# A four-token decode block in one pass: a bf16 turn for the last group, a norm without helper tiles, a projection by columns and half-row loads in two parts

## The chip, the cores and the metric

The kernel runs on one core of a Trainium2 chip. The metric is the device time in microseconds (us) of one execution. TensorE (PE in the profile) multiplies matrices, PEld is its loading of weights, DVE is VectorE, ACT is ScalarE, POOL is GpSimd, and SP issues nearly all transfers from device memory (HBM) into the on-chip memory (SBUF).

## What is computed

Four tokens (B=4, one position each) with D=448 go through the same two blocks twice:

```python
x = x + A(layernorm(x));  x = x + F(layernorm(x))
x = x + A(layernorm(x));  x = x + F(layernorm(x))

def A(x):      # 16 query heads, 8 K/V heads, Dh = 256, window of the last 2048 positions
    q = (x @ wq).reshape(B, Sq, Hq, Dh).transpose(0, 2, 1, 3)
    k = repeat(k_cache[:, :, Sk - W:, :], 2, axis=1)     # W = 2048; v alike
    p = softmax(einsum("bhqd,bhkd->bhqk", q, k) * Dh ** -0.5)
    return einsum("bhqk,bhkd->bhqd", p, v) ... .reshape(B, Sq, Hq * Dh) @ wo

def F(x):      # width 1792
    return (silu(x @ w_gate) * (x @ w_up)) @ w_down
```

Weights and caches are bf16 and the same for both layers. A K or V window of one token and one K/V head is 1 MB. All of them, with the weights, make 103.9 MB.

## The kernel before

**Data.** K and V come in units of 512 KB (half a window) into 34 slots of SBUF. What a list named HOLD names stays there for layer 1; the rest is loaded a second time. A list named WHOLE says which K windows come as one transfer of 1 MB instead of two. SLOTS gives the slot of each unit. wq lies in slots that become free for K and V when the last query projection is done. `load` issues the weights; the last 64 rows of wq, gate and up (rows 384 to 447) are read with `"r (h c) -> (r h) c"`: half h of row r goes to partition 2r+h, in one transfer of 128 partitions.

**Tokens and stages.** Tokens don't go through the layers together. A plan of 38 stages says which (token, layer, K/V head) are worked on next, mostly pairs of groups, so that one token's FFN and next query projection run while another token's windows stream in. A group is named by these three numbers: 312 is token 3, layer 1, head 2, the last one.

**A group** (`group`): DVE transposes K in blocks (`tr`, L856), PE computes the scores (L890) with a query that POOL has masked (`qe`, L896), DVE takes the maximum (L906), PE spreads it over partitions (L911), ACT computes the exponentials (L924), PE turns them (L937), ACT copies them (L946), PE sums them (`tot`, L954), DVE (L959) and POOL (L981) make the reciprocals, PE multiplies with V (`pv`, L968, 32 matmuls of 256 columns). Then o is turned: ACT copies it in bf16 (`oh`, L995), DVE writes high minus low parts (`oho`, L997), PE turns it with two bf16 matmuls (`flip`, L1003), and DVE divides (`oT`, L1013). The last group alone takes another way: ACT copies in fp32 (`ohf`, L984), and PE turns with two fp32 matmuls (`flipf`, L989, four passes in the trace).

**Output projection** (`out_proj`): by rows (`opr`, L1033), four matmuls of 448 columns into bank A, or by columns (`opc`, L1025), sixteen of one column for each token. The stages that finish a token take columns, the others rows. When a token is done, `rows` copies the rows of bank A out (`rowcp`, L773), adds and turns them with eight fp32 matmuls (`rturn`, L778) and a zero matmul (`clear`, L529), and `residual` adds to x.

**Norm** (`norm`, L532 to L561), 16 times: DVE sums the squares (`nv`), PE sums over partitions into Z2 (`nstat`, L541), DVE subtracts the mean (`nxn`, L545) and copies the statistics (`ncp`, L547), POOL computes the scale. For the 64 last features, PE multiplies column 3 of xn with a tile that doubles each partition (`nxe`, L549, tile `twice`), and DVE masks the result into xe (`nxe2`, L552, tile `par`): partition 2r+h holds feature 384+r in half h.

**Query projection** (`qproj`) and FFN follow on a norm. In the FFN by columns, gate and up (`guc3` with xn, `guc1` with xe, L720) go through ACT and DVE into `downc` (L756), which ends with a `clear` (L529).

**Order.** Each engine's order is written out by hand in SEQ_PE, SEQ_DVE, SEQ_ACT, SEQ_POOL and SEQ_SP, as numbers of operations. A "w1" in SEQ_PE is a filler: a matmul of zeros, 512 columns wide, into bank A (L1112). Planned durations (DUR) serve to place waits only. 317 fillers stand in PE's order.

**The tail.** After the last V window: PE's order is scores 312, pv 311, flip 310, spread 312, filler, opc 310, turn 312, flip 311, nxe of token 1, tot 312, filler, opr 311, pv 312, rturn 3, flipf 312, nstat of token 2, opc, nstat of token 3, filler, nxe of token 3, then the FFN of the last tokens by columns, and the output (`orow`, `ocp`, two small transfers).

Of the kernel before, what the change touches and what calls it, by code (L numbers as in the profile page):

```python
# [85 lines left out]
)  # L86
SEQ_DVE = (
# [21 lines left out]
)  # L109
SEQ_ACT = (  # L110
# [66 lines left out]
class Graph:  # L177
# [45 lines left out]
    def dma(self, nbytes, emit, sem, r=(), w=(), cells=(), run=4096):  # L223
        o = self.op(SP, "ld", emit, r=r, w=w)
        o.nbytes, o.cells, o.run = nbytes, cells, run
        if not cells:
            self._count(o, sem)
# [951 lines left out]
```

## Time and profile before

| what | value |
|---|---|
| median of three runs | 282.47 us (280.79 to 282.82) |
| profiled execution | 281.3 us |
| its span, first to last instruction | 279.4 us |
| mean granted TensorE clock | 0.964 |
| PE busy | 256.0 us (92%), 4796 matmuls |
| of it L1112 (fillers) | 96.2 us, 317 times, 399 ns each |
| DVE busy | 179.5 us (64%) |
| ACT, POOL busy | 61.8 us, 80.3 us |
| read from HBM | 103.91 MB, 372 GB/s over the span |

Busy times say how much an engine did, not that it was the bound; for that one looks at which wait ends last in a stretch. The profile shows a granted clock of 1.00 or 0.50 for TensorE in each stretch; a share in between is a mix of the two. A line's mean duration mixes both.

### The profile page before, as it was taken

What the parts mean: (1) busy time and instruction counts of PE and PEld (TensorE: products, weight loads), DVE (VectorE), ACT (ScalarE), POOL (GpSimd) and SP (SyncE); (2) the same over time, 40 slices, a digit from 0 to 9 for tenths busy, and PEclk for the clock granted to TensorE, in tenths of its full rate; (3) what the DMA queues carried; (4) which work ended last, traced back from release to release, by engine and by line L of the source; (5) the groups of instructions that cost most, each with busy time, mean ns of one, the idle gap of its engine ahead of it and who ended that gap; (6) DMA issues with size and microseconds to landing.
All of it is one profiled execution on the core that took longest, in us unless ns stands there. A gap on an engine that the chain in (4) does not pass through costs nothing. (4 is left out here: it accounts for less than half of the span.)

```text
span 279.4 us, 10832 instructions
## 1 busy us (share of the span) xinstructions
PE 256.0 (92%) x4796; PEld 149.3 (53%) x4796; DVE 179.5 (64%) x548; ACT 61.8 (22%) x173; POOL 80.3 (29%) x225
## 2 busy tenths in 40 slices
PE   3899799999999999999998889999998999999995
PEld 1333344334775554545555445655764577576684
DVE  4388644634603789668766978793898858489421
ACT  0003010101113222232223123134213212423301
POOL 1033230011121534315232333243153242423430
PEclk9999989999999999999999999999999999989857
DMA  7999999999999999999999999999999999999200
GB/s 282 428 419 420 413 409 409 395 394 406 401 394 409 396 412 410 412 401 361 409 401 420 418 412 409 393 369 412 414 420 402 405 400 382 392 414 412 115 2 2
DMA packets 26894, 104.61 MB, mean 374 GB/s; under 512 B 2652, under 2 KB 6752, under 8 KB 22880
## 3 DMA queue, kind: packets, MB, share of 16 engines
q1 hardware_dynamic: 26839, 103.92, 93.5%
q8 instruction: 37, 0.61, 0.9%
q14 instruction: 10, 0.07, 0.1%
q10 hardware_dynamic: 8, 0.00, 0.0%
HBM read 103.91 MB, written 0.00 MB: 372 GB/s over the span
## 5 line engine op out<-in xcount | busy, mean ns | idle before, releaser
L856 DVE STREAM_TRANSPOSE half<-half 128x1024 uint32<-128x1024 uint32 x88 | 106.6, 1228 | 9.3 <-DMA half<-in_A_k_cache_dram 9.2
L1112 PE MATMUL A<-identb,small 128*128 128x512 bf16 x317 | 96.2, 399 | 4.4 <-DVE A L424 4.4
L981 POOL TENSOR_TENSOR small<-small 128x2 f32<-128x2 f32 (+1 forms) x48 | 38.5, 804 | 54.1 <-DVE small L959 54.1
L968 PE MATMUL Y<-half,pT 128*8 128x256 bf16 (+1 forms) x1024 | 45.7, 281 | 3.1 <-DMA half<-in_A_v_cache_dram 1.0
L890 PE MATMUL S<-half,qe 128*8 128x128 bf16 (+1 forms) x1536 | 43.5, 241 | 0.6 <-DVE half L856 0.2
L1112 PEld LDWEIGHTS A<-identb,small 128*128 128x128 bf16 x317 | 27.6, 104 | 29.9 <-issue 12.5
L890 PEld LDWEIGHTS S<-half,qe 128*8 128x8 bf16 x1536 | 30.8, 85 | 10.9 <-issue 1.6
L924 ACT ACTIVATE po<-S,small 104x128 bf16<-104x128 f32 (+1 forms) x48 | 19.3, 402 | 68.7 <-DVE small L920 66.6
L896 POOL TENSOR_TENSOR qe<-qc,tiny 128x64 bf16<-128x64 bf16 x64 | 17.9, 292 | 45.6 <-PE S L890 29.1
L997 DVE SCALAR_TENSOR_TENSOR po<-po,small,Y 128x256 bf16<-128x256 bf16 x47 | 22.0, 468 | 13.3 <-ACT po L995 13.2
L968 PEld LDWEIGHTS Y<-half,pT 128*8 128x8 bf16 (+1 forms) x1024 | 20.3, 85 | 17.6 <-issue 6.9
L995 ACT ACTIVATE po<-Y 128x256 bf16<-128x256 f32 x47 | 18.0, 383 | 48.1 <-PE Y L968 33.2
L906 DVE TENSOR_REDUCE tiny<-S 104x1 bf16<-104x128 f32 (+1 forms) x48 | 15.6, 326 | 11.5 <-PE S L890 11.2
L557 POOL TENSOR_SCALAR st<-st 128x1 f32<-128x1 f32 x16 | 4.2, 264 | 58.5 <-DVE st L547 52.5
L946 ACT ACTIVATE pT<-Y 128x64 bf16<-128x64 f32 (+1 forms) x48 | 12.2, 258 | 27.8 <-PE Y L937 27.7
L1033 PE MATMUL A<-wo_sb,oT 128*4 128x448 bf16 x188 | 16.4, 353 | 0.9 <-DVE oT L1013 0.9
L920 DVE TENSOR_REDUCE small<-S 104x1 f32<-104x32 f32 x48 | 8.6, 180 | 10.4 <-PE S L914 8.3
L1013 DVE TENSOR_TENSOR oT<-Y,small 128x4 bf16<-128x4 f32 (+1 forms) x63 | 8.9, 153 | 7.7 <-PE Y L989 4.6
L911 PE MATMUL S<-small,identb 104*104 104x32 bf16 x48 | 10.1, 210 | 3.4 <-DVE small L459 2.0
L1060 POOL MEMSET oT<- 128x16 bf16 x38 | 4.1, 111 | 29.9 <-PE A L1033 23.2
L959 DVE TENSOR_REDUCE small<-Y 128x2 f32<-128x32 f32 (+1 forms) x48 | 9.2, 191 | 5.0 <-PE Y L954 4.8
L778 PE MATMUL Z<-small,wide 128*128 128x1 f32 (+1 forms) x80 | 10.9, 249 | 0.5 <-ACT wide L773 0.5
(136 smaller groups left out, 268.0 us busy)
## 6 DMA issues: line engine op xcount, KB each, us to landing
half<-in_A_v_cache_dram SPq DMA_DIRECT2D x87, 512.0 KB, 10.6
half<-in_A_k_cache_dram SPq DMA_DIRECT2D x28, 1024.0 KB, 10.6
half<-in_A_k_cache_dram SPq DMA_DIRECT2D x32, 512.0 KB, 6.7
wo_sb<-in_A_wo_dram SPq DMA_DIRECT2D x8, 448.0 KB, 13.5
half<-in_A_wq_dram SPq DMA_DIRECT2D x3, 1024.0 KB, 12.3
wd_sb<-in_B_w_down_dram SPq DMA_DIRECT2D x1, 1568.0 KB, 20.2
wg_sb<-in_B_w_gate_dram SPq DMA_DIRECT2D x1, 1344.0 KB, 15.7
wu_sb<-in_B_w_up_dram SPq DMA_DIRECT2D x1, 1344.0 KB, 17.8
```

Of the source, the lines that this page charges most:

```text
L856: return e.transpose(a, a)
L890: last = e.matmul(Sb[s_][qd:qd + 8, 0:32 * 2 * J], lhsT=qe[q_][:, P, ce, :, :].rearrange("p a n -> p (a n)"), rhs=keys(kcs[P], J * x, J, c ...
L896: g.op(POOL, "qe", lambda e, P=P, t=t, kvh=kvh: e.tensor_tensor(qe[q_][:, P, :, :, :], qc[t][:, kvh, :, :].unsqueeze(2).broadcast_to([128, ...
L906: g.op(DVE, f"max{n}", lambda e: e.tensor_reduce(pmax[s_][0:R, :], Sb[s_][0:R, 0:N], AX.X, ALU.max), r=(f"s{s_}",), w=(f"pmax{s_}",), bank ...
L924: return e.activation(praw[0:R, 0:128 * n].rearrange("p (g r l) -> p g r l", g=2 * n, l=2), Sb[s_][0:R, 0:128 * n].rearrange("p (l g r) -> ...
L946: g.op(SCA, f"pt{n}", lambda e: e.activation(pf, Yb[p_][:, 0:PW], ACT.Copy), r=(f"yp{p_}",), w=(f"pT{pt}",), bank=(f"Y{p_}",))
L968: last = e.matmul(Yb[p_][32 * gg:32 * gg + M, 256:512], lhsT=pT[pt][:, gg, 2 * a + hv, 4 * P:4 * P + M] if n == 2 else p1[:, gg % 2, 2 * a ...
L981: g.op(POOL, f"pow{n}", lambda e: e.tensor_tensor(ri[p_][:, 0:2 * n], rs[p_][:, 0:2 * n], expo[:, 1:1 + 2 * n], op=ALU.pow), r=(f"rs{p_}", ...
L995: g.op(SCA, "oh", lambda e: e.activation(oh[:, :], Yb[p_][:, 256:512], ACT.Copy), r=(f"y{p_}",), w=("oh",), bank=(f"Y{p_}",))
L997: g.op(DVE, "oho", lambda e: e.scalar_tensor_tensor(out=oh[:, :], in0=oh[:, :], scalar=lomask[:, 0:1], in1=Yb[p_][:, 256:512], op0=ALU.mul ...
L1033: last = e.matmul(Ab[32 * k:32 * k + B, 0:D], lhsT=oT[oi][:, k % 2, k // 2, :], rhs=wo_sb[:, 4 * kvh + k, :], start=False, stop=False, ski ...
L1112: return e.matmul(Ab[:, 0:512], lhsT=zero[:, 0:1].broadcast_to([128, 128]), rhs=identb[:, :].unsqueeze(1).broadcast_to([128, 4, 128]), sta ...
```

## The change

1. **o of the last group.** `ohf` and `flipf` are gone, and the last group takes `oh`, `oho` and `flip` like the others.
2. **Norm.** `nxe` and `nxe2` are gone from all 16 norms, with the tiles `twice` and `par`. DVE writes xe itself with two instructions (`nx1`, `nx2`) of 64 partitions and one column each, from x and Z2: feature 384+r in half h is now on partition 64h+r. xn has three columns. On the last norm DVE's order is nxn, ncp, nx1, nx2.
3. **Half rows.** To fit this, the last 64 rows of wq, gate and up are loaded as two transfers of 64 partitions each, one after the other on SP.
4. **Second-last stage** projects by columns (`opc`) instead of rows (`opr`).
5. **Query projection.** `qs` now masks and widens on DVE (128 columns for each token, before 32), and `qsel` takes 4 matmuls instead of 16.
6. **clear** stands first in `downc` and in the turn of x at the start, with start=True.
7. **Lists.** HOLD has v331 for v360, WHOLE has 106 and 112 for 001 and 110; SLOTS and all orders are written anew. SP's order of loads is else the same, and so are the bytes. SEQ_PE has 264 fillers. In the tail of PE's order, a filler stands behind spread 312, two behind flip 311, none behind tot 312; opr 311 is opc 311.

```diff
@@ load
+            if isinstance(src, tuple):
+                g.dma(nbytes, lambda e: [e.dma_start(dst[64 * h:64 * h + 64], src[h]) for h in range(2)], f"w{nw[0]}",
+                      w=(key,), run=run, parts=2)
...
+        def halves(src, n):
+            return src[384:448, 0:n], src[384:448, n:2 * n]
...
-        load(1 << 19, wq_sb[:, 3 * 4096:], A_wq[384:448, :].rearrange("r (h c) -> (r h) c", h=2), "wq3", 4096)
+        load(1 << 19, wq_sb[:, 3 * 4096:], halves(A_wq, 2048), "wq3", 4096)
...
-                load(229376, wsb[:, 3 * FF:], src[384:448, :].rearrange("r (h c) -> (r h) c", h=2), nm + "b", 1792)
+                load(229376, wsb[:, 3 * FF:], halves(src, 896), nm + "b", 1792)
@@ norm
-            vec("nxn", lambda e: e.tensor_scalar(xn[:, :, t], x[:, t, :], Z2[:, 0:1], None, op0=ALU.subtract),
+            vec("nxn", lambda e: e.tensor_scalar(xn[:, :, t], x[:, t, 0:3], Z2[:, 0:1], None, op0=ALU.subtract),
...
-            g.op(PE, "nxe", lambda e: e.matmul(Z2[:, 16:17], lhsT=twice[:, :],
-                                                    rhs=xn[:, 3, t:t + 1], start=True, stop=True, skip_group_check=True),
-                 r=(f"xn{t}", "twice"), w=("z2",), bank=("Z2",))
-            vec("nxe2", lambda e: e.tensor_tensor(xe[:, :, t], par[:, :], Z2[:, 16:17].broadcast_to([128, 2]), op=ALU.mult),
-                ("z2", "par"), (f"xe{t}",), ("Z2",))
+            for h in range(2):
+                vec(f"nx{1 + h}", lambda e, h=h: e.tensor_scalar(
+                    xe[64 * h:64 * h + 64, h, t:t + 1], x[64:128, t, 3:4], Z2[64:128, 0:1], None, op0=ALU.subtract),
+                    (f"x{t}", "z2"), (f"xe{t}",), ("Z2",))
@@ qproj
-            vec("qs", lambda e: e.tensor_copy(qS[:, 0:32 * n], Zb[:, 0:32 * n]), ("z",), ("wa",), ("Z",))
+            vec("qs", lambda e: e.tensor_tensor(
+                qS[:, 0:128 * n].rearrange("p (k c x) -> p k c x", c=4, x=4),
+                Zb[:, 0:32 * n].rearrange("p (k x) -> p k x", x=4).unsqueeze(2).broadcast_to([128, 8 * n, 4, 4]),
+                qmask[:, :].unsqueeze(1).unsqueeze(3).broadcast_to([128, 8 * n, 4, 4]), op=ALU.mult),
...
-                for c in range(4):
-                    for a in range(4):
-                        o = Z2[32 * a:32 * a + 32, 0:128 * n].rearrange("p (k c x) -> p k c x", c=4, x=4)[:, :, c, :]
-                        last = e.matmul(o, lhsT=identb[:, 32 * c:32 * c + 32], rhs=src, start=(c == 0), stop=(c == 3),
-                                        skip_group_check=True)
+                for a in range(4):
+                    last = e.matmul(Z2[32 * a:32 * a + 32, 0:128 * n], lhsT=rep32[:, :], rhs=qS[:, 0:128 * n], start=True,
+                                    stop=True, skip_group_check=True)
@@ group
-            if final:
-                g.op(SCA, "ohf", lambda e: e.activation(ohf[:, :], Yb[p_][:, 256:512], ACT.Copy), r=(f"y{p_}",),
-                     w=("oh", "praw"), bank=(f"Y{p_}",))
...
-                g.op(PE, "flipf", flipf, r=("oh", "praw", "oself"), w=(f"yp{p_}",), bank=(f"Y{p_}",))
@@ stages
-                out_proj(oi, ts, kvh, bool(full))
+                out_proj(oi, ts, kvh, bool(full) or si + 2 == len(plan()))
```

More of the change, by code (lines that the diff above doesn't have):

```diff
@@ L53 @@
 SEQ_PE = (
[32 rows of a table removed]
[29 rows of a table added]
 )
 SEQ_DVE = (
[21 rows of a table removed]
[21 rows of a table added]
 )
 SEQ_ACT = (
[8 rows of a table removed]
[8 rows of a table added]
 )
 SEQ_POOL = (
[9 rows of a table removed]
[9 rows of a table added]
 )
 SEQ_SP = (
[7 rows of a table removed]
[7 rows of a table added]
 )
 SLOTS = (
[4 rows of a table removed]
[4 rows of a table added]
 )
 DUR = dict(
-    i0=.24, i1=.5, fill0=.98, mz=.49, d1=.17, d2=.27, nstat=.45, nxe=.18, rv1=.19, rv2=.33, qmm3=1.2, qmm1=.5, qcp=.69,
-    qturn=.25, qsel=.28, rvh=.24, rvt=.28, gur3=1.2, gur1=.7, tanhr=.69, fturn=.26, downr=.93, ohf=.38, flipf=.42, fh=.23, ft=.29, guc3=1.26,
-    guc1=.6, tanhc=.27, downc=1.65, rowcp=.54, rturn=.35, orow=.25, xin=.26, tr=1.24, qe=.29, sc1=.85, sc2=1.5, sch=1.2, max1=.29,
+    i0=.24, i1=.5, fill0=.98, mz=.49, d1=.17, xcp=.17, d2=.27, nstat=.45, rv1=.19, rv2=.33, qmm3=1.2, qmm1=.5, qcp=.69,
+    qturn=.25, qsel=.25, rvh=.24, rvt=.28, gur3=1.2, gur1=.7, tanhr=.69, fturn=.26, downr=.93, fh=.23, ft=.29, guc3=1.26,
+    guc1=.4, tanhc=.27, downc=1.7, rowcp=.54, rturn=.4, orow=.25, xin=.26, tr=1.24, qe=.29, sc1=.85, sc2=1.5, sch=1.2, max1=.29,
     max2=.42, spread=.3, negm=.18, exp1=.36, exp2=.47, turn1=.26, turn2=.35, pt1=.22, pt2=.33, tot1=.19, tot2=.23,
     sum1=.18, sum2=.23, pv=.5, pow1=.7, pow2=1.0, oh=.38, oho=.47, flip=.2, oT=.16, opc=.56, opr=.45, oz=.11, nw=.16,
-    nv=.16, nxn=.23, ncp=.15, nxe2=.15, qs=.2, qc=.28, ffa=.68, ffb=.75, fht=.18, fca=.23, fcb=.23, fcw=.22, st=.1, fx=.15, rowsub=.62,
+    nv=.16, nxn=.2, ncp=.15, nx1=.15, nx2=.15, qs=.2, qc=.28, ffa=.68, ffb=.75, fht=.18, fca=.23, fcb=.23, fcw=.22, st=.1, fx=.15, rowsub=.62,
     rowadd=.15, resid=.15, oxb=.16, ocp=.25, ng1=.26, ng2=.3, ng3=.57, fw=.45, ld=.05)
@@ L221, in op, with dma @@
         return o
-    def dma(self, nbytes, emit, sem, r=(), w=(), cells=(), run=4096):
+    def dma(self, nbytes, emit, sem, r=(), w=(), cells=(), run=4096, parts=1):
         o = self.op(SP, "ld", emit, r=r, w=w)
@@ L226, in dma, with _count @@
         if not cells:
-            self._count(o, sem)
+            self._count(o, sem, parts)
         return o
-    def _count(self, o, sem):
+    def _count(self, o, sem, parts=1):
         o.dsem = sem
-        self.dcount[sem] = self.dcount.get(sem, 0) + 16
+        self.dcount[sem] = self.dcount.get(sem, 0) + 16 * parts
         o.dval = self.dcount[sem]
@@ L355, in build @@
         identb = sb("identb", [128, 128], BF16)
-        twice = sb("twice", [128, 128], BF16)
-        tiny = sb("tiny", [128, 16 + NS], BF16)
-        onesb, qmask, osel, rsel = tiny[:, 0:1], tiny[:, 2:6], tiny[:, 6:10], tiny[:, 10:14]
-        par = tiny[:, 14:16]
-        pmax = [tiny[:, 16 + s:17 + s] for s in range(NS)]
-        tsel = sb("tsel", [128, 4, B], BF16)
+        rep32 = sb("rep32", [128, 32], BF16)
+        tiny = sb("tiny", [128, 14 + NS], BF16)
+        onesb, qmask, osel = tiny[:, 0:1], tiny[:, 2:6], tiny[:, 6:10]
+        pmax = [tiny[:, 14 + s:15 + s] for s in range(NS)]
+        tsel = identb[:, :].rearrange("p (j x) -> p j x", j=4)[:, :, 0:B]
         selt = [sb(f"selt{h}", [128, 4, 12], BF16) for h in range(2)]
@@ L427, in build @@
         XN = tuple(f"xn{t}" for t in range(B))
-        g.op(DVE, "fill0", c_fill, w=("onesf", "expo", "qmask", "zero") + XN +
+        g.op(DVE, "fill0", c_fill, w=("onesf", "expo", "qmask", "zero") + XE +
              tuple(f"acc{t}" for t in range(B)) + tuple(f"row{t}" for t in range(B)), bank=("A",))
@@ L528, in clear @@
         def clear(e, out, m):
-            return e.matmul(out, lhsT=zero[:, 0:1].broadcast_to([128, 64]), rhs=identb[:, 0:m], start=False, stop=True,
-                            skip_group_check=True)
+            return e.matmul(out, lhsT=zero[:, 0:1].broadcast_to([128, 64]), rhs=identb[:, 0:m], start=True, stop=False,
+                     skip_group_check=True)
         def norm(t, x, summed=True):
-            s, si, k = st[:, t, :], sti[:, t, :], f"st{t}"
+            s, k = st[:, t, :], f"st{t}"
             if not summed:
@@ L752, in down @@
                 k, last = 0, None
+                clear(e, Zb[0:64, 3 * cw:4 * cw], cw)
                 for cc in range(4):
@@ L759, in down @@
                         k += 1
-                return clear(e, Zb[0:64, 3 * cw:4 * cw], cw)
+                return last
             g.op(PE, "downc", down, r=WIDE + ("wd", "zero"), w=("z",), bank=("Z",))
@@ L799, in x_in @@
         def x_in(e):
+            clear(e, Zb[0:64, 12:16], 4)
             for cc in range(4):
                 q = 64 * (cc // 3)
-                e.matmul(Zb[q:128, 4 * cc:4 * cc + 4], lhsT=xio[0:B, 128 * cc:128 * cc + 128 - q], rhs=identb[0:B, 0:B],
+                last = e.matmul(Zb[q:128, 4 * cc:4 * cc + 4], lhsT=xio[0:B, 128 * cc:128 * cc + 128 - q], rhs=identb[0:B, 0:B],
                          start=(cc == 0), stop=(cc == 3), skip_group_check=True)
-            return clear(e, Zb[0:64, 12:16], 4)
+            return last
         g.op(PE, "xin", x_in, r=xio_k + ("identb", "zero"), w=("z",), bank=("Z",))
-        g.op(DVE, "d1", lambda e: e.tensor_copy(xs[:, :, :], Zb[:, 0:16].rearrange("p (c t) -> p t c", t=B)),
+        g.op(DVE, "xcp", lambda e: e.tensor_copy(xs[:, :, :], Zb[:, 0:16].rearrange("p (c t) -> p t c", t=B)),
              r=("z",), w=tuple(f"xs{t}" for t in range(B)) + tuple(f"x{t}" for t in range(B)), bank=("Z",))
@@ new lines, in group, with flip @@
+            g.op(SCA, "oh", lambda e: e.activation(oh[:, :], Yb[p_][:, 256:512], ACT.Copy), r=(f"y{p_}",),
+                 w=("oh",), bank=(f"Y{p_}",))
+            g.op(DVE, "oho", lambda e: e.scalar_tensor_tensor(
+                out=oh[:, :], in0=oh[:, :], scalar=lomask[:, 0:1], in1=Yb[p_][:, 256:512], op0=ALU.mult,
+                op1=ALU.subtract), r=(f"y{p_}", "oh", "lomask"), w=("oh",), bank=(f"Y{p_}",))
+            def flip(e):
+                for dh in range(2):
+                    last = e.matmul(Yb[p_][:, 2 * n * dh:2 * n * dh + 2 * n],
+                                    lhsT=oh[:, :].rearrange("p (m e) -> p e m", e=2)[:, dh, :],
+                                    rhs=osel[:, 0:2 * n], start=dh == 0, stop=dh == 1, skip_group_check=True)
+                return last
@@ L1008, in group @@
+            g.op(PE, "flip", flip, r=("oh", "osel"), w=(f"yp{p_}",), bank=(f"Y{p_}",))
             yo = Yb[p_][:, 0:4 * n].rearrange("p (d P n) -> p d P n", d=2, n=2)
```

74 lines of the change are left out of this document (22 added, 52 removed), and 161 rows, old and new, of tables (HOLD, SEQ_ACT, SEQ_DVE, SEQ_PE).

## The prediction

> **What bounds the kernel now.** I read the page's sums and slices first, then stretches of the trace, then the chain of work at the end, and last the waits. In the first fence the slices are 7 us long: the digit in the line DMA is the load of the 16 transfer engines, PEclk the granted TensorE clock.
>
> ```profile
> span 279.4 us, 10832 instructions
> PE 256.0 (92%) x4796; PEld 149.3 (53%) x4796; DVE 179.5 (64%) x548; ACT 61.8 (22%) x173; POOL 80.3 (29%) x225
> ...
> PEclk9999989999999999999999999999999999989857
> DMA  7999999999999999999999999999999999999200
> ...
> HBM read 103.91 MB, written 0.00 MB: 372 GB/s over the span
> ```
>
> The transfer engines are full from the first slice to the 37th; then come about 18 us without them. So the time is the stream of 103.91 MB (at the 410 GB/s of the next fence 253 us), plus a head, plus the tail after the last load. PE's 92% is no bound, since part of it is the filler matmul of L1112, work without a result. The stretches below give busy time of PE, PEld, DVE, ACT, POOL, then clock, DMA share and GB/s.
>
> ```profile
> 124.00:132.00 8.00, 7.67 (x156) 4.09 (x157) 6.88 (x19) 1.76 (x5) 3.07 (x11) 1.00 1.00 362
> 180.00:188.00 8.00, 7.38 (x143) 4.28 (x146) 7.42 (x17) 2.23 (x6) 4.20 (x12) 1.00 0.97 363
> 188.00:236.00 48.00, 45.61 (x1016) 29.99 (x1005) 35.18 (x99) 12.53 (x37) 16.52 (x47) 1.00 1.02 408
> 236.00:240.00 4.00, 4.00 (x70) 2.02 (x66) 1.80 (x14) 1.07 (x2) 1.33 (x4) 1.00 0.94 350
> 245.90:249.30 3.40, 3.29 (x70) 2.85 (x73) 2.46 (x15) 1.50 (x4) 0.25 (x2) 1.00 0.99 411
> 249.30:252.80 3.50, 3.50 (x88) 2.70 (x84) 3.50 (x5) 0.38 (x1) 1.68 (x5) 0.51 1.02 416
> 259.00:260.00 1.00, 1.00 (x44) 0.87 (x40) 0.26 (x3) 0.00 (x0) 0.00 (x0) 1.00 1.03 401
> 260.00:261.00 1.00, 0.98 (x29) 0.60 (x18) 0.87 (x5) 0.38 (x1) 0.12 (x1) 1.00 0.37 148
> 259.60:263.00 3.40, 2.84 (x66) 1.90 (x58) 2.08 (x13) 1.19 (x3) 0.93 (x2) 1.00 0.25 96
> 263.00:266.40 3.40, 3.40 (x45) 2.52 (x41) 0.02 (x1) 0.93 (x2) 1.90 (x4) 0.50 0.02 5
> 269.80:273.20 3.40, 3.40 (x85) 2.94 (x86) 0.46 (x3) 0.58 (x3) 1.57 (x5) 0.50 0.02 5
> 273.20:276.60 3.40, 2.66 (x82) 2.35 (x78) 0.77 (x4) 0.26 (x1) 0.00 (x0) 0.99 0.01 2
> ```
>
> Three things are to be seen. The stream falls to 362, 363 and 350 GB/s in three places: 8 x (1 - 362/410) + 8 x (1 - 363/410) + 4 x (1 - 350/410) = 2.4 us that compute, which frees slots late, takes from it. The stream ends at about 260.4, so the tail is 279.4 - 260.4 = 19 us. And TensorE works at half clock from 263.0 to 273.2, for most of that tail, though PE was busy for 2.84 of the 3.40 us before. The tail's chain, instruction by instruction:
>
> ```profile
> 262.43 0.18 PE L549 MATMUL Z<-xn,twice 128*128 128x1 bf16 x1 [0.44 <-issue]
> 262.52 0.38 PE L1112 MATMUL A<-identb,small 128*128 128x512 bf16 x1
> 262.83 0.43 PE L1033 MATMUL A<-wo_sb,oT 128*4 128x448 bf16 x4
> 263.07 1.90 PE L968 MATMUL Y<-half,pT 128*8 128x256 bf16 x32
> 264.90 1.64 PE L778 MATMUL Z<-small,wide 128*128 128x1 f32 x7
> 265.01 0.38 ACT L984 ACTIVATE po<-Y 128x256 f32<-128x256 f32 x1 [1.16 <-PE Y L968]
> 266.57 1.01 PE L989 MATMUL Y<-small,po 128*128 128x4 f32 x4
> 270.79 0.19 PE L549 MATMUL Z<-xn,twice 128*128 128x1 bf16 x1
> 270.84 1.28 PE L720 MATMUL Z<-xn,wg_sb 128*128 128x30 bf16 x42
> 275.99 0.20 PE L529 MATMUL Z<-identb,small 128*64 128x30 bf16 x1
> ```
>
> The last group's PV ends at 265.0, rturn (L778) of token 3 keeps PE until about 266.6, and only then does flipf (L989, four fp32 passes) start. The output projection waits for it through oT.
>
> **The change part by part.** The sum is made against the profiled execution (281.3 us by the clock, 279.4 span, so 1.9 around it). It lies 1.2 us under the median of 282.47 and inside the three runs' 280.79 to 282.82.
>
> *o of the last group in bf16.* flipf goes (1.01). In its place come the usual oh (ACT), oho (DVE) and flip (two bf16 matmuls). Their prices:
>
> ```profile
> L997 DVE SCALAR_TENSOR_TENSOR po<-po,small,Y 128x256 bf16<-128x256 bf16 x47 | 22.0, 468 | 13.3 <-ACT po L995 13.2
> L1003 PE MATMUL Y<-tiny,po 128*128 128x2 bf16 (+1 forms) x94 | 9.3, 168 | 0.3 <-DVE po L997 0.2
> ```
>
> ACT takes 0.38 either way (row at 265.01). oho adds 0.47, from 265.4 to about 265.9, and is hidden by rturn up to 266.6; if rturn ran at full clock (about 0.7 us less) it would still just be hidden. The flip pair costs between one and two of L1003's 168 ns, 0.17 to 0.34, depending on how far they overlap; I take the middle, 0.26. Gain 1.01 - 0.26 = 0.75. Without the cover it would be 0.75 - 0.47 = 0.28; I take 0.75.
>
> *norm.* nxe (L549) and nxe2 (L552) go from all 16 norms, and two DVE instructions of one column come in (nx1, nx2). On the last norm, guc3 (L720) reads xn only, and nxe stands between: it began 0.05 us behind nxe, and ncp stands ahead of nxn now and behind it no more. What the path can win is at most nxe's 0.19 and at least nothing; I take 0.12. nx1 and nx2, 2 x 0.15 by nxe2's row below, end long before the second guc1 reads xe, 1.4 us later. In the other 15 norms DVE no longer stands still for PE:
>
> ```profile
> L552 DVE TENSOR_TENSOR st<-tiny,Z 128x2 bf16<-128x2 bf16 x16 | 2.4, 149 | 5.7 <-PE Z L549 5.7
> ```
>
> That is 5.7 us of idle time before its 16 instructions, and queued behind each are the K transposes (L856) which feed the scores. It counts only where DVE is what frees slots, the three dips: between 0 and 1.5 us, of which I take 0.
>
> *Second-last projection by columns.* opr (four matmuls, 0.43 in the row at 262.83) becomes opc (sixteen, N=1). Half of the 32 matmuls of the last two projections took 1.47/2 = 0.74 at half clock; 0.67 at full clock (both rows below). So +0.24 against opr's 0.43, on the path: pv of the last group stands behind it. The filler between tot2 and that projection is gone (0.31 from its start to the next row's), and two stand earlier, behind flip of 311, where PE waited 0.44 us anyway. Together -0.0 to +0.3; I take +0.05. rowcp of token 3 now waits for opc, 0.2 later, under pv (1.90).
>
> ```profile
> 260.77 0.67 PE L1025 MATMUL A<-oT,wo_sb 128*128 128x2 bf16 x16
> ...
> 267.87 1.47 PE L1025 MATMUL A<-oT,wo_sb 128*128 128x1 bf16 x32
> ```
>
> *clear first.* In downc the zero matmul (L529, 0.20) moves ahead of the others, whose h comes 0.3 us behind the last guc. It has the same operands to wait for; -0.1 at most if PE overlaps it, 0 otherwise. I take -0.1.
>
> *Query projection.* The diff also has qsel with 4 matmuls for 16 and a wider qs. Off the tail, four or five times; 0.
>
> *Half rows.* The last 64 rows of wq, gate and up are each loaded with two transfers of 64 partitions: 512 + 224 + 224 KB, the same bytes and lengths of rows. In the stream's 410 GB/s they take 1.28 + 0.56 + 0.56 = 2.4 us. If both parts run beside each other and beside the next loads, it costs 0 (SP gets three more issues, and is some 16 us ahead of the landings here); if each goes at half rate, it costs another 2.4.
>
> ```profile
> half<-in_A_wq_dram SPq DMA_DIRECT2D x1, 512.0 KB, 15.9
> wu_sb<-in_B_w_up_dram SPq DMA_DIRECT2D x1, 224.0 KB, 17.7
> ```
>
> I take 0: the last column is the time from issue to landing, and 16 to 18 us for loads of about 1 us says that some ten others are in the queue. [...]
>
> *Order and fillers.* Every order is written anew. In PE's order stand 264 fillers, before 317; about 45 of the 53 fall away ahead of the first scores of layer 1, most of them between 60 and 150 us. In the 3.4 us ahead of 263.0 there would be three where the row at 262.52 is the only one.
>
> ```profile
> 150.00:245.90 95.90, 22.98 (x69) 5.93 (x69) 1.00 1.01 403
> 245.90:279.40 33.50, 1.36 (x3) 0.49 (x3) 0.76 0.45 179
> ```
>
> These rows are L1112's alone. Where they stand close, the clock is 1.00 throughout; with three in 33 us it is 0.76. What this does to the time is the matter of two rivals; here 0.
>
> Sum: 281.3 - 0.75 - 0.12 + 0.05 - 0.1 = 280.4.
>
> **The rivals.**
>
> *The clock stays up in the tail, and the switches get shorter.* For it: 1.90 us for the last PV against 1.05 for an earlier one, 1.64 against 0.96 for the seven matmuls of rturn, 0.56 against 0.38 for nstat, twice.
>
> ```profile
> 242.55 1.05 PE Y L968 x32
> 257.87 0.96 PE L778 MATMUL Z<-small,wide 128*128 128x1 f32 x7
> 255.42 0.38 PE L541 MATMUL Z<-st,small 128*128 128x2 f32 x2
> 267.44 0.56 PE L541 MATMUL Z<-st,small 128*128 128x2 f32 x2
> ```
>
> That is 0.85 + 0.68 + 0.36 = 1.9, and 2.0 with the two projections. Fillers of 512 columns are what differs between the stretches that kept the clock and those that lost it; three ahead of 263.0 could hold it. With 0.5 of the 5.7 us that DVE waits: 280.4 - 2.0 - 0.5 = 277.9. Against it: the stretch from 263 on has no filler of its own, so the drop may only come 3.4 us later. [...]
>
> *Too few fillers in the middle (slower).* The 53 fillers that are gone held the clock between 60 and 240 us. A stretch of PV and scores without them lost it (249.30, above). At full clock PE was busy for 95% of 188 to 236, and about 24% of its time was fillers: 3.40 x 0.95 = 3.2 us of work, and at half clock 3.4 us do about 1.9 of it (1.05 against 1.90 for PV). Each lost stretch sets PE back by 1.3 us. It counts where slots come free late, the three dips, which are 20 us or six stretches long; four of the six make 5.2: 280.4 + 5.2 = 285.6. Against it: at 249.30 the stream ran on at 416 GB/s through half a clock. The rival decides from the second lost stretch in a dip: 280.4 + 2.6 = 283.0 is above the median of before.
>
> *Half rows at half rate.* 280.4 + 2.4 = 282.8, on the median of before; the change would then do nothing to the time. Against it the queue in the row of the wq load.
>
> **How the numbers follow.** Chances: forecast 0.40, clock held 0.27, fillers 0.20, half rate 0.13. About 1%, 2.8 us, is what a measurement of this kernel tells from no change. The forecast's own range is 278.9 (DVE's 1.5) to 282.3 (the median's lead of 1.2, and 0.28 for 0.75, and 0.3 for the projection). The range reaches to the clock rival with 0.9 more for the switches (277.0) and to the filler rival with a little room (286.0). Against before's 282.5, faster by over 1% is below 279.7: the clock rival and a fifth of the forecast, 0.34. Slower is above 285.3: most of the filler rival and what adds up with half rate, 0.24 with what a wholly rewritten order can lose in places that I cannot price. The rest is 0.42.
>
> **What would show it.** Right: the last flip takes about 0.2 us behind rturn, with oho ended before it; no L549; the stream ends at 260.4 within a microsecond; the tail is 18 us. The clock rival shows in the row from 263.0 on at 1.00. The filler rival shows as 0.50 in PEclk between 60 and 245 with less GB/s in the same stretch, and the stream's end behind 262. Half rate shows in a hole in GB/s near 19 us. Wrong outright: a stream that ends over 2 us earlier or later, since nothing in the sum moves it.

## The result, and the profile after

The changed kernel takes 293.90 us (293.01 to 295.06, four runs), the kernel before 282.64 (280.79 to 284.15) beside it: a ratio of 1.040, with a 95% interval of 1.033 to 1.048. It is 11.3 us slower. The forecast was 280.4 in a range from 277.0 to 286.0; the result lies above the range. Times are medians of all executions of a run, while ratios leave out executions in a slower state of the chip, so a ratio need not be the quotient of the two times beside it.

The page of the profiled execution after (the sums, then the slices, of 7.3 us here):

```profile
span 291.4 us, 10609 instructions
PE 253.9 (87%) x4677; PEld 144.3 (50%) x4677; DVE 188.9 (65%) x560; ACT 62.0 (21%) x173; POOL 80.5 (28%) x225
...
PEclk9998999999968999598699799999999999997975
DMA  7999999999999899986999999999999999999600
GB/s 280 427 313 418 410 414 367 387 342 402 404 392 386 342 416 414 411 333 225 317 329 417 415 369 418 411 329 388 401 414 405 409 407 393 385 405 412 245 3 0
...
HBM read 103.91 MB, written 0.00 MB: 357 GB/s over the span
```

The same bytes come at 357 instead of 372 GB/s. The line GB/s has dips of several kinds: at the third slice, at the seventh and ninth, and from the 18th to the 21st, where the DMA digit falls to 6. The clock is lost in four places between 80 and 165 us, where it was whole before. The stretches (columns as in the prediction):

```profile
17.00:18.00 1.00, 0.00 (x0) 0.00 (x0) 1.00 (x1) 0.00 (x0) 0.00 (x0) 1.00 1.03 291
18.00:19.00 1.00, 0.60 (x4) 0.44 (x5) 0.51 (x4) 0.00 (x0) 0.00 (x0) 1.00 0.99 184
19.00:20.00 1.00, 0.45 (x3) 0.00 (x0) 1.00 (x4) 0.00 (x0) 0.80 (x4) 1.00 0.99 213
20.00:21.00 1.00, 0.56 (x10) 0.23 (x12) 0.95 (x4) 0.00 (x0) 1.00 (x3) 0.87 0.99 246
48.00:50.00 2.00, 2.00 (x10) 0.78 (x8) 2.00 (x2) 0.00 (x0) 0.00 (x0) 1.00 1.08 284
62.00:64.00 2.00, 1.77 (x18) 0.68 (x19) 0.00 (x0) 0.00 (x0) 0.00 (x0) 1.00 1.07 287
84.00:88.00 4.00, 3.97 (x22) 1.81 (x22) 0.40 (x2) 0.50 (x3) 0.00 (x0) 0.50 1.06 410
124.00:128.00 4.00, 3.77 (x85) 1.99 (x83) 1.71 (x9) 1.35 (x5) 2.43 (x5) 1.00 0.81 281
128.00:132.00 4.00, 3.05 (x74) 1.72 (x73) 2.95 (x7) 0.88 (x4) 0.70 (x1) 1.00 0.89 353
132.00:136.00 4.00, 3.79 (x57) 2.31 (x46) 3.46 (x8) 1.31 (x5) 0.00 (x0) 1.00 0.56 173
136.00:140.00 4.00, 4.00 (x70) 2.27 (x69) 2.58 (x11) 0.62 (x3) 2.19 (x9) 0.60 0.99 322
192.00:196.00 4.00, 4.00 (x93) 2.39 (x92) 3.29 (x13) 1.09 (x4) 2.29 (x9) 1.00 0.88 285
```

Two kinds of loss are to be told apart by the DMA share. At 17 to 21, 48 and 62 us the engines are busy all the time (0.99 to 1.08) and still move 184 to 291 GB/s: the transfers themselves are slow. At 124 to 136 the share falls to 0.56: there the queue runs empty, since slots were freed late: SP stands for 13.9 us, up to 124.80, until scores (L883) free a slot.

Where the time goes is best seen by the stream: at what time so many MB have landed, worked out from the landings of all loads. The table gives the time before, and how much later each kernel is in its profiled execution (the runs are described below):

| MB landed | before, at us | after | e6 | e5 | e3 | e13 | e1 | e2 | e14 |
|---|---|---|---|---|---|---|---|---|---|
| 25 | 64.9 | 4.1 | 3.4 | 0.2 | 4.0 | 0.6 | 0.1 | 4.1 | 0.3 |
| 46 | 117.5 | 4.9 | 3.4 | 0.6 | 4.0 | 3.1 | 1.1 | 6.7 | 5.3 |
| 58 | 147.3 | 12.5 | 4.3 | 2.5 | 5.4 | 3.9 | 5.1 | 11.4 | 7.6 |
| 79 | 200.1 | 14.0 | 4.1 | 4.1 | 9.4 | 3.2 | 8.2 | 13.1 | 12.8 |
| 103 | 260.2 | 13.1 | 3.9 | 6.5 | 10.6 | 7.3 | 9.7 | 17.3 | 14.9 |

After 25 MB, when all half rows are in, the changed kernel is 4.1 us behind; 7.6 more are lost between 46 and 58 MB; then little (1.5 by 79 MB, of which 0.9 comes back). Its last V lands at 275.48 (262.36 before). From there the tail takes 15.96 us, 17.07 before. So 13.1 - 1.1 = 12.0 us, which is the difference of the spans. The tail of after:

```profile
276.99 1.05 PE L961 MATMUL Y<-half,pT 128*8 128x256 bf16 x32
277.97 0.98 PE L770 MATMUL Z<-small,wide 128*128 128x1 f32 x7
278.51 0.48 DVE L978 SCALAR_TENSOR_TENSOR po<-po,small,Y 128x256 bf16<-128x256 bf16 x1 [1.30 <-ACT po L976]
279.05 0.20 PE L984 MATMUL Y<-tiny,po 128*128 128x4 bf16 x2
282.37 1.30 PE L711 MATMUL Z<-xn,wg_sb 128*128 128x30 bf16 x42
286.10 2.16 PE L748 MATMUL Z<-wide,wd_sb 128*128 128x30 bf16 x56
```

The last PV and rturn run at full clock now (1.05 and 0.98 us, 1.90 and 1.64 before). The flip takes 0.20 where flipf took 1.01. The clock falls at 280.1 instead of 263.0, so that downc comes into the slow part (2.16; before it had the clock at 1.00 and took 1.78, from 274.49 to 276.27).

### The profile page after: what moved, and what is told of

The parts are those of the page before. It is cut to its first block, busy times and chain, and to the rows that moved or that the text cites. A ratio compares the mean times of both kernels' runs of the same rounds, so it can differ in the third digit from the quotient of the medians.

```text
span 291.4 us, 10609 instructions
## 1 busy us (share of the span) xinstructions
PE 253.9 (87%) x4677; PEld 144.3 (50%) x4677; DVE 188.9 (65%) x560; ACT 62.0 (21%) x173; POOL 80.5 (28%) x225
## 4 chain that ended last, share of the span: by engine, by line
PE 42%; DMA 18%; DVE 18%; SPq 12%; issue 4%; ACT 3%; POOL 2%; DVEq 0%; ACTq 0%
DVE half L849 9%; PE Y L961 8%; PE A L1093 7%; DMA half<-in_A_v_cache_dram 7%; DMA wu_sb<-in_B_w_up_dram 6%; PE S L883 6%; SPq L859 6%; DMA half<-in_A_k_cache_dram 5%; SPq L837 3%; PE Z L770 3%; PE A L1006 2%; SPq L488 2%; DVE po L978 2%; PE A L1014 2%; PE Z L748 2%
## 5 line engine op out<-in xcount | busy, mean ns | idle before, releaser
L1093 PE MATMUL A<-identb,small 128*128 128x512 bf16 x264 | 83.0, 411 | 4.6 <-DVE A L419 4.6
L961 PE MATMUL Y<-half,pT 128*8 128x256 bf16 (+1 forms) x1024 | 46.3, 282 | 2.9 <-issue 1.3
L883 PE MATMUL S<-half,qe 128*8 128x128 bf16 (+1 forms) x1536 | 44.3, 244 | 4.3 <-POOL qe L889 1.6
L1093 PEld LDWEIGHTS A<-identb,small 128*128 128x128 bf16 x264 | 24.0, 105 | 28.8 <-issue 13.4
L883 PEld LDWEIGHTS S<-half,qe 128*8 128x8 bf16 x1536 | 30.9, 86 | 14.2 <-POOL qe L889 2.9
L978 DVE SCALAR_TENSOR_TENSOR po<-po,small,Y 128x256 bf16<-128x256 bf16 x48 | 22.7, 473 | 17.7 <-ACT po L976 17.5
L961 PEld LDWEIGHTS Y<-half,pT 128*8 128x8 bf16 (+1 forms) x1024 | 18.9, 84 | 16.7 <-issue 8.0
L899 DVE TENSOR_REDUCE tiny<-S 104x1 bf16<-104x128 f32 (+1 forms) x48 | 15.4, 325 | 11.5 <-PE S L883 11.4
L1014 PE MATMUL A<-wo_sb,oT 128*4 128x448 bf16 x184 | 17.3, 363 | 2.5 <-DMA wo_sb<-in_A_wo_dram 1.2
L984 PE MATMUL Y<-tiny,po 128*128 128x2 bf16 (+1 forms) x96 | 9.8, 170 | 3.0 <-issue 1.5
L984 PEld LDWEIGHTS Y<-tiny,po 128*128 128x128 bf16 x96 | 6.3, 99 | 12.0 <-DVE po L978 5.7
```

Of the source, the lines that this page charges most:

```text
L883: last = e.matmul(Sb[s_][qd:qd + 8, 0:32 * 2 * J], lhsT=qe[q_][:, P, ce, :, :].rearrange("p a n -> p (a n)"), rhs=keys(kcs[P], J * x, J, c ...
L961: last = e.matmul(Yb[p_][32 * gg:32 * gg + M, 256:512], lhsT=pT[pt][:, gg, 2 * a + hv, 4 * P:4 * P + M] if n == 2 else p1[:, gg % 2, 2 * a ...
L978: g.op(DVE, "oho", lambda e: e.scalar_tensor_tensor(out=oh[:, :], in0=oh[:, :], scalar=lomask[:, 0:1], in1=Yb[p_][:, 256:512], op0=ALU.mul ...
L984: last = e.matmul(Yb[p_][:, 2 * n * dh:2 * n * dh + 2 * n], lhsT=oh[:, :].rearrange("p (m e) -> p e m", e=2)[:, dh, :], rhs=osel[:, 0:2 * ...
L1014: last = e.matmul(Ab[32 * k:32 * k + B, 0:D], lhsT=oT[oi][:, k % 2, k // 2, :], rhs=wo_sb[:, 4 * kvh + k, :], start=False, stop=False, ski ...
L1093: return e.matmul(Ab[:, 0:512], lhsT=zero[:, 0:1].broadcast_to([128, 128]), rhs=identb[:, :].unsqueeze(1).broadcast_to([128, 4, 128]), sta ...
```

## The experiments

Three theories: A, the two-part half rows; B, clock lost because fillers are missing; C, the new orders, lists and slots themselves. From the third run on there is D, the new operations. A ratio is against the kernel before in the same series, with its 95% interval.

| run | what | us | before | ratio |
|---|---|---|---|---|
| e1 | after, half rows whole | 291.51 | 281.34 | 1.036 (1.030 to 1.043) |
| e2 | after, fillers back | 297.60 | 281.34 | 1.055 (1.047 to 1.062) |
| e3 | new operations, old orders | 289.97 | 281.34 | 1.032 (1.026 to 1.037) |
| e4 | before, fewer fillers | 289.44 | 281.34 | none, see there |
| e5 | e3, half rows whole | 286.91 | 282.83 | 1.017 (1.009 to 1.026) |
| e6 | before, half rows in two | 285.32 | 282.83 | 1.013 (1.006 to 1.020) |
| e7 | e3, half rows by ACT's queue | 291.14 | 282.83 | 1.030 (1.022 to 1.039) |
| e8 | e1, fillers back | 291.51 | 282.83 | 1.034 (1.027 to 1.040) |
| e9 | before, new norm | 283.17 | 281.96 | 1.006 (1.002 to 1.010) |
| e10 | before, new qs and qsel | 282.75 | 281.96 | 1.004 (1.000 to 1.008) |
| e11 | before, new tail | 285.12 | 281.96 | 1.012 (0.998 to 1.026) |
| e12 | the same again | 283.19 | 283.30 | 1.000 (0.996 to 1.004) |
| e13 | old operations, new orders | 286.53 | 280.78 | 1.016 (1.007 to 1.024) |
| e14 | e13, fillers back | 293.54 | 280.78 | 1.045 (1.037 to 1.053) |

In e1, e5, e6, e8 and e9 the loaded half rows lie as in one kernel and xe as in the other, so these kernels leave out the matching of the two; the amounts and kinds of work stay.

**e1: the half rows whole again.**

```diff
-        load(1 << 19, wq_sb[:, 3 * 4096:], halves(A_wq, 2048), "wq3", 4096)
+        load(1 << 19, wq_sb[:, 3 * 4096:], A_wq[384:448, :].rearrange("r (h c) -> (r h) c", h=2), "wq3", 4096)
...      # gate and up alike
```

> The changed kernel, with the last 64 rows of wq, gate and up each in one transfer of 128 partitions again (rows interleaved as before, so what xe meets in these rows is not the matching half; amounts, rows and times of all other work stay). In the changed kernel's trace the stream falls to 184-291 GB/s in the 3.5 us of the wq pair and to about 290 in those of the gate and up pairs, and it is 4.1 us behind after them. Theory A (the transfers of 64 partitions go at half rate): the stream isn't behind at 67 us and the time falls by at least 4 us, to 290 or less; if the later dips (90-100, 124-152, 192-200 us) came from the lateness too, to 283. Theory B (the dips come from lost clock, as fillers are missing): 289.5 to 290.5, with the dips still there. Theory C (the new orders are the cause of everything): no change, 294.

The stream is not behind any more after 25 MB (0.1 us): the 4.1 us there are the half rows'. But the time falls only from 293.9 to 291.5 (by the ratios from 1.040 to 1.036, inside the noise). A dip at 124 to 135 us stays, smaller (4.0 us are lost between 46 and 58 MB, 7.6 in the changed kernel), and it stays with the clock whole:

```profile
126.00:129.00 3.00, 2.82 (x26) 1.86 (x30) 2.81 (x7) 0.87 (x3) 0.00 (x0) 1.00 0.70 224
129.00:132.00 3.00, 2.91 (x79) 2.04 (x75) 1.90 (x12) 0.50 (x2) 0.88 (x5) 1.00 0.81 276
```

**e2 and e8: fillers back**, in the changed kernel and in e1.

```diff
 SEQ_PE: 57 "w" more, each as far ahead as needed for the old count in front of every operation
```

> The changed kernel with 57 fillers put back into PE's order, so that ahead of each operation there are at least as many as before. Theory B (lost clock): PEclk is 1.00 from 60 to 245 us, the dips at 90-100, 124-152 and 192-200 us shrink, and the time falls by 5 to 8 us to 286-289; the first 67 us stay 4 us behind. Theory C (the orders themselves leave slots late, whatever the clock): the clock is back, the dips stay, 293 to 295. Theory A alone: 294 as well, or 286 if lateness and clock only matter together.

> The changed kernel with half rows in one transfer each (291.5 us alone) and 57 fillers put back (297.6 with the two-part loads). Theory B (lost clock): 284 to 288, the clock whole from 60 to 245. Theory C (new orders leave slots late): the dip at 124-135 us stays though the clock is whole there, 291 to 295.

e2 is slower than the changed kernel (1.055 against 1.040). In its profiled execution the clock is lost at 84 to 88 as without them, and the dip comes again, with the clock whole (4.7 us between 46 and 58 MB):

```profile
84.00:88.00 4.00, 3.97 (x22) 1.77 (x22) 0.40 (x2) 0.50 (x3) 0.00 (x0) 0.50 1.06 412
124.00:140.00 16.00, 15.35 (x286) 8.50 (x288) 10.35 (x35) 4.18 (x14) 4.64 (x13) 1.00 0.83 303
```

e8 has the same time as e1, and its dip at 126 to 132 has a clock of 1.00 as well (247 and 266 GB/s). So lost clock is not the cause of the 4 to 5 us of the dip that stay with a clock of 1.00. The changed kernel loses some 3 us more there, beside two stretches at half clock (116 to 123 and 137 to 144 us); whether the clock took these is open. As the cause of the whole loss, B falls.

**e3 and e5: the new operations in the old orders**, once with half rows in two parts and once whole.

```diff
 # HOLD, WHOLE, SLOTS and all SEQ_* of before, renumbered;
 # nx1, nx2 in the place of nxe2, oho ahead of the last oT
```

> All operations of the changed kernel (bf16 turn, norm on DVE, projection by columns, qs and qsel, half rows in two transfers), but each engine's order, the fillers, the residency lists and the slots of the kernel before. Theory A: 4.1 us behind from the half rows, 1 us won in the tail: 285 to 286.5. Theories B and C (fillers or orders make the rest): the same 285 to 286.5, so the remaining 8 us are the orders' or fillers'. If one of the other new operations is the cause: above 290.

> All new operations in the orders, lists and slots of the kernel before, as the run with the old orders, but the half rows again in one transfer of 128 partitions each (rows interleaved, so xe meets rows of another half). That run was 4.1 us behind after the half rows and lost 4 to 5 more at about 180 us and 1 at 245. Theory A (the half rows are the cause, and the later dip is their lateness: PE comes to a K that isn't there, idles, loses its clock): 280 to 282.5, no dip. Rival D (one of the other new operations, qs and qsel above all, makes the dip at 180): 285 to 287, with the dip still there.

e3 has no dip like that at 124 to 136 us (4.0 us behind at 46 MB, 5.4 at 58): it comes only with the new orders. e3 loses 4 us more at 180 to 190. e5 loses 2.9 us there (1.2 behind at 70 MB, 4.1 at 79), with hardly any lateness before it. These rows are e5's:

```profile
180.00:184.00 4.00, 4.00 (x95) 2.68 (x92) 3.17 (x12) 0.37 (x2) 0.27 (x1) 1.00 0.85 301
184.00:188.00 4.00, 3.36 (x83) 1.71 (x80) 3.73 (x7) 1.44 (x4) 1.92 (x8) 1.00 0.87 310
```

In the kernel before, the same place has 351 and 375 GB/s:

```profile
180.00:184.00 4.00, 3.63 (x84) 2.01 (x83) 3.45 (x7) 1.44 (x4) 2.13 (x9) 1.00 0.94 351
184.00:188.00 4.00, 3.74 (x67) 2.27 (x63) 3.96 (x11) 0.78 (x2) 2.07 (x3) 1.00 1.00 375
```

So what is left in e5 is neither the half rows' nor the orders': theory A's part about later dips falls, D stands with 1.017.

**e4: the kernel before with fewer fillers.**

```diff
 SEQ_PE of before: 57 "w" less
```

> The kernel before with 57 fillers taken out, so that ahead of each operation there are at most as many as in the changed kernel; nothing else. Theory B: stretches with the clock at 0.50 between 60 and 245 us, 4 to 8 us slower, 286.5 to 290.5. Theory C: the clock may fall, but the slots come free in time: 282 to 284. Theory A: 282.5.

Its four times are 281.94, 285.58, 293.30 and 303.53 us, at mean clocks of 0.954, 0.942, 0.911 and 0.728. In the old order the missing fillers cost much or nothing, and the lower the clock was, the longer the time. No verdict comes of four such times.

**e6: the half rows in two parts, in the kernel before.**

```diff
+                g.dma(nbytes, lambda e: [e.dma_start(dst[64 * h:64 * h + 64], src[h]) for h in range(2)], ...)
```

> The kernel before, with the last 64 rows of wq, gate and up each in two transfers of 64 partitions (halves one after the other, so xe meets rows of another half); nothing else. Theory A: the stream is 4.1 us behind from 67 us on, so at least 285.5, and with the later dips 287 to 290. Rival D: 285.5 and no dip at 180. If the half rate only comes with the new orders: 282.

3.4 us behind after 25 MB, 3.9 at the end, and no dip that the kernel before hasn't: the lateness stays what it is. 1.29% of 282 us is 3.6 (by the interval, 1.7 to 5.6). Its stretch of the wq pair, and the same stretch of the kernel before:

```profile
17.00:21.00 4.00, 1.17 (x14) 0.44 (x15) 2.98 (x8) 0.00 (x0) 3.59 (x10) 1.00 1.03 280
...
17.00:21.00 4.00, 3.41 (x27) 1.45 (x25) 3.85 (x11) 0.00 (x0) 2.33 (x7) 1.00 1.02 412
```

**e7: the same transfers from another queue.**

```diff
-                g.dma(nbytes, lambda e: [e.dma_start(...) for h in range(2)], ..., parts=2)
+                o = g.op(SCA, "st", lambda e: [e.dma_start(...) for h in range(2)], w=(key,))
```

> All new operations in the old orders, half rows in two transfers of 64 partitions, but these six are issued by ACT (wq's two at the start, the other four behind ACT's second operation), so that they run beside the queue of SP instead of in it. [...] If each such transfer costs its 4.1 us wherever it runs: 289 to 291 as with the old orders.

It is not faster than e3 (1.030 and 1.032), and in its trace the stream is 3.3 us behind after 25 MB, 4.0 in e3. The wq pair now runs beside SP's whole transfers, and both are slow, though the engines are never idle (the kernel before has 428, 418 and 430 GB/s in these three stretches):

```profile
4.00:6.00 2.00, 2.00 (x5) 0.70 (x6) 0.77 (x5) 0.00 (x0) 0.00 (x0) 1.00 1.05 364
6.00:8.00 2.00, 2.00 (x6) 0.53 (x4) 0.00 (x0) 0.00 (x0) 0.00 (x0) 1.00 1.01 254
8.00:10.00 2.00, 0.91 (x8) 0.56 (x9) 1.30 (x13) 0.00 (x0) 0.00 (x0) 1.00 1.03 326
```

In SP's queue 184 to 291 GB/s went with these transfers, where 412 went before. That the transfers of the other queue don't make up the rest is shown by the 254 above. No run separates the 64 partitions from the other thing that is new in these loads, that each reads one half of every row and skips the other.

**e9 and e10: the new norm, and the new query selection, each alone in the kernel before.**

```diff
 # e9:  - nxe, nxe2   + nx1, nx2        # e10: - qs (copy), qsel (16)   + qs (mask, widen), qsel (4)
```

> The kernel before with the new norm alone (nx1 and nx2 on DVE in the place of nxe2, no nxe; half rows loaded whole as before, so xe meets rows of another half). All new operations in the old orders, with whole half rows, took 286.9 us against 282.8: 4 us that are neither the half rows nor the new orders. Theory D1 (the norm is it: nx1 and nx2 take 227 ns each where nxe2 took 149, 4.9 us more of DVE in 16 norms, and at the token switches DVE has no spare time): 284.5 to 287, the stream behind at 175-190 us. Rival D2 (qs, 0.29 instead of 0.19 us and 0.69 instead of 0.25, is it): 281 to 283. Rival D3 (nothing of it; runs of this kernel differ by chance when the clock drops): 282 here and in the next.

> The kernel before with the new query selection alone (qs masks and widens on DVE, qsel with 4 matmuls). D1: 281 to 283. D2: 284.5 to 287. D3: 282.

The norm costs 0.6% (1.6 us); the selection 0.4%, not told from nothing (its interval reaches 1.000). Together 1.0%, in the lower part of e5's interval; the other 0.7% of e5 is assigned to nothing. Rows of the changed kernel for them:

```profile
L542 DVE TENSOR_SCALAR xe<-xr,Z 64x1 bf16<-64x1 f32 x24 | 5.4, 227 | 0.6
L609 DVE TENSOR_TENSOR wide<-Z,tiny 128x128 bf16<-128x128 f32 (+1 forms) x5 | 1.9, 372 | 5.1 <-PE Z L602 5.0
```

An instruction of one column takes 227 ns, twice in each norm (eight of the 32 stand in a row of their own), where nxe2 took 149: 16 x (2 x 227 - 149) = 4.9 us more of DVE. qs takes 372 ns in the mean of its five times, two widths mixed.

**e11 and e12: the new tail alone in the kernel before.**

```diff
-            if final: ...ohf, flipf...
+            oh, oho, flip for the last group; opc in the second-last stage; fillers as in the changed kernel's tail
```

> The kernel before with the tail of the change alone: bf16 turn of the last group, second-last projection by columns, one filler behind the last spread and two behind the flip of 311 in the place of the one behind tot. In the changed kernel the tail from the last V's landing to the end took 15.96 us, before 17.07, with the last PV at 1.05 us instead of 1.90. If that gain is the tail's own: 281 to 281.8, 1.0 less than before, the clock whole until about 280 less 10 us. [...]

> The same kernel as the run before with the tail of the change alone, once more in more rounds, since its times there lay between 279.4 and 289.5 us. Its profile had the last V's landing at 262.29 us (262.36 before) and 15.26 us from there to the end (17.07 before), with TensorE's clock whole until the FFN of the last tokens. If the tail's gain is its own: 1.2 to 1.8 us less than before, 280 to 281.5. [...]

In the two profiles the tail takes 15.26 and 14.89 us, 17.07 before. But the time is not measurably less (1.000, 0.996 to 1.004), and the short tail isn't the edit's: with flipf in it, the tail takes 14.47 us in e4's trace and 14.86 in e9's, where the clock fell as late. Of the 1.2 to 1.8 us that e12 was to gain, if the tail's gain were its own, nothing came. The two profiled executions of this one kernel also show why one trace misleads: the last V lands at 262.29 us in the one and at 268.10 in the other. The second lost 5.7 us of its stream, nearly all at 175 to 195, where the clock fell:

```profile
180.00:185.00 5.00, 5.00 (x90) 3.13 (x88) 3.02 (x12) 0.33 (x2) 0.00 (x0) 0.58 0.82 294
185.00:190.00 5.00, 5.00 (x93) 2.47 (x86) 3.93 (x8) 1.44 (x4) 2.18 (x9) 0.74 0.88 295
```

No kernel of this study is measurably faster than the one before.

**e13 and e14: old operations in the new orders**, with 264 fillers and with 321.

```diff
 # HOLD, WHOLE, SLOTS and all SEQ_* of the changed kernel, renumbered;
 # nxe ahead of the next instruction that needs its bank
```

> All operations and transfers of the kernel before (fp32 turn, norm over PE, rows in the second-last stage, half rows whole), in the orders, lists and slots of the changed kernel with its 264 fillers; nxe stands ahead of the next instruction that needs its bank. Theory C or B: 286 to 289 (1.5 to 2.5% slower), the stream behind at 124-150 us by 4 to 5 us. If the new orders only cost with the new operations in them: 281 to 284.

> The same with fillers put back so that ahead of each operation there are at least as many as before. Theory B: 281 to 284, the clock whole. Theory C: 286 to 289 as without them.

e13 is 1.6% slower: the new orders cost by themselves (C). But the place isn't the one expected: it loses 2.5 us between 25 and 46 MB and 3.5 between 91 and 97 MB, less than 1 at the dip of the changed kernel. So where the loss falls isn't a property of the orders alone. One thing is common to the kernels with the new orders: SP waits longer at that place for PE to free slots. Two issues of SP in the kernel before, then the same two loads (the 53rd and the 56th of K and V) in e13 and in e1:

```profile
115.75 0.33 SPq L844 DMA_DIRECT2D half<-in_A_k_cache_dram  x1
122.93 4.18 SPq L850 DMA_DIRECT2D half<-in_A_k_cache_dram  x4
...
118.86 0.33 SPq L844 DMA_DIRECT2D half<-in_A_k_cache_dram  x1
126.28 4.13 SPq L850 DMA_DIRECT2D half<-in_A_k_cache_dram  x4
...
118.61 0.33 SPq L837 DMA_DIRECT2D half<-in_A_k_cache_dram  x1
126.02 4.13 SPq L843 DMA_DIRECT2D half<-in_A_k_cache_dram  x4
```

Some 3 us later, with the old operations as with the new; in e5, with the old orders, it is 116.44 and 123.45. e13, already 3.1 us behind at 46 MB, is 3.9 behind at 58; e1, 1.1 behind, comes to 5.1. In the changed kernel they are issued at 124.80 and 132.20, 6.2 us behind e1: more than the 4.1 of the half rows.

With fillers put back e13's kernel is 4.5% slower instead of 1.6, though the clock of the profiled execution is higher (0.961 against 0.940; in the mean of four executions 0.954 against 0.949). B falls here, too. That the fillers' own time stands in the way in these orders is argued, not shown.

## Why the prediction was wrong, point by point

By its own sign the prediction is wrong outright: the stream's end, which nothing in its sum moves, came 13.1 us later. Three terms that it put at 0 (half rows, new operations, orders) make up the loss, as far as the ratios below tell. Even its two slow rivals together, 280.4 + 2.4 + 5.2 = 288.0, fall 5.9 us short.

The three parts measured alone multiply to 1.013 x 1.017 x 1.016 = 1.047, inside the interval of the result (1.033 to 1.048). Two at a time they fit as well: 1.030 for e3's 1.032, 1.033 for e1's 1.036. In us of before: some 3.6 half rows, 4.9 operations, 4.4 orders. The sum of 12.9 is 1.6 above the 11.3 measured, no more than the intervals allow.

- **The sum of the tail: the turn was priced right, the total came out by luck.** oho ended at 278.99, before rturn (279.01), so its cover held; the flip took 0.20 (forecast 0.26), opc 0.66 (0.67). But the -0.9 forecast and the -1.1 measured are made of different things. PV began 1.51 us behind the last V's landing, where it had been 0.71, and only 0.05 of that was in the sum. PV and rturn then ran 0.85 and 0.66 us faster, by a clock that the sum had left out, and at the end the clock stayed down. Other tails show that the turn doesn't decide: 14.47 (e4), 14.86 (e9) and 14.78 (e14) with flipf, 16.92 (e1), 16.74 (e3) and 17.49 (e5) with the bf16 turn. They are short where PV begins soon (0.5 to 0.8 us after the landing) and the clock holds.
- **"I take 0" for the half rows: the step that failed first.** The bounds were 0 and 2.4; it cost 4.1 in the trace and 3.6 in e6. The evidence for 0 was a long queue of transfers, and the long queue did not help while the engines were busy and slow (share 0.99 to 1.03 at 184 to 291 GB/s). The upper bound was too low as well: the wq pair lost 2.3 us where 1.28 was the bound, and gate and up 1.8 where it was 1.12; why it is more than a halved rate is not shown. That each part goes at half rate, from which the bound of 2.4 was made, no run shows; the runs showed 184 to 291 GB/s where 412 went before.
- **"of which I take 0" for the norm, "Off the tail, four or five times; 0" for the query selection.** The norm was priced by the wait that went (5.7 us of DVE) and by a row of 149 ns, as a gain or nothing. The new instructions took 227 ns, and the norm alone cost 0.6% in e9: the wait that went was worth less than the 4.9 us of DVE that came. That they cost where DVE has the least to spare (7.42 busy of 8.0 at 180 to 188) fits e5's loss at that place and is argued only. All new operations cost 1.7% in e5.
- **"here 0" for the orders.** 1.6% in e13. By the row-by-row costing of operations this was not to be seen; a rewritten order had a share of the slower chance only as "places that I cannot price".
- **The filler rival: right in its sign, its mechanism not borne out.** The clock did fall in four places, and 285.6 was its price; but giving the fillers back cost 1.4% in e2, 2.9% in e14 and nothing in e8, and e1 and e8 lose 4 us at the dip with a clock of 1.00. Of the 53 fillers, 11 and not about 45 fall away ahead of the first scores of layer 1 in PE's order; 45 is reached at the scores of group 302.
- **The clock rival: half of it came.** The clock held through PV and rturn; it was lost 4.7 us after the last V's landing instead of 0.6, as the prediction had said against it. That the three fillers ahead did this is not shown: in e9, with the old fillers, it held for 6.2 us. And the reading that fillers are what differs between stretches that keep the clock and those that lose it was wrong already on the trace of before. L1112 alone, in three stretches there:

```profile
30.90:34.30 3.40, 0.82 (x3) 0.34 (x4) 1.00 1.05 423
252.80:256.20 3.40, 0.00 (x0) 0.00 (x0) 1.00 1.03 410
259.60:263.00 3.40, 0.38 (x1) 0.10 (x1) 1.00 0.25 96
```

The clock was at 0.50 behind the first and the third, and at 1.00 behind the second, which has no filler.

- **Half rows at half rate, given 0.13**, was the one rival whose sign and place the trace bore out (the dip at 17 to 21 us), at more than its price.

What stays open: which instruction makes the new orders free their slots late, and whether it is the orders or the lists and slots, which no run separates. In e1 and in the changed kernel one candidate shows, argued only. DVE stands for a flip at its turn in the queue, with the next transpose of K behind it:

```profile
110.04 0.18 PE L984 MATMUL Y<-tiny,po 128*128 128x4 bf16 x1 [1.49 <-issue]
110.26 0.17 DVE L994 TENSOR_TENSOR oT<-Y,small 128x4 bf16<-128x4 f32 x1 [1.66 <-PE Y L984]
```

These rows are e1's; in the changed kernel the same pair of matmuls is 1.48 us apart. e8 has only 0.53 there and the same dip, so this stall alone isn't it.

## What to carry to other kernels

The transfers of 64 partitions were to be priced by their rate with the engines busy (184 to 291 GB/s), not by whether a queue hides their latency: in this kernel, bound by its stream, the 3.4 us lost on them in e6 were never made up. Where a hand-written order is balanced against the stream, an edit is best priced by the engine that has least to spare at the stage in question (here, it seems, DVE at the token switches), and a wholly rewritten order is a change of its own, to be tried apart from the operations. Shortening the tail by 1 to 2 us in a trace is not a gain yet, when the stream's end moves by more than that from one execution to the next (5.8 us between the traces of e11 and e12), and the tail itself from one trace to another (14.47 to 17.49 us).

## What the runs showed of the hardware that was not expected

- With two transfers of 64 partitions in a full queue the stream fell to 184 to 291 GB/s in the changed kernel (412 before), and beside them in a second queue it fell as well (254 in e7, 418 before).
- PE stopped inside a run of matmuls that waited for nothing the profile shows ("issue" in the rows above), for 0.4 to 1.9 us. Counted over the 16 traces, 37 stops of over 0.4 us lie at the same place of a block of 128 recorded matmuls (0.53 to 0.69 of it), and each ends 1.25 to 1.6 us after a packet of 16 KB on the queue marked "instruction" has landed: 1.26 and 1.39 us in the kernel before (up to 157.32 and 262.43), 1.38, 1.35 and 1.40 us in the changed one (up to 108.14, 114.48 and 262.94). (Nine others, at 18 to 21 us, come before the first such packet.) The page of the changed kernel has 36 such packets:

```profile
q8 instruction: 36, 0.59, 0.8%
```

What PE waited for in these stops no run shows. The kernel before had two such stops, of 0.71 and 0.44 us (the second is the wait of nxe in the prediction's tail), the others from none (e9) to four (e1, with 4.3 us in all).
- More filler matmuls came with a higher clock, and not with a shorter time. In the mean of the executions compared, the clock with 57 more rose from 0.929 to 0.947 (e2, 1.4% slower), from 0.937 to 0.961 (e8, the same time) and from 0.949 to 0.954 (e14, 2.9% slower).
